# A softmax without its maximum, checked on chip, with a general program behind a branch

## The chip, the cores and the metric

The kernel runs on one core of a Trainium2 chip. A core has a matrix engine (TensorE; PE in the profile, with PEld for its weight loads), a vector engine (VectorE, DVE), an activation engine (ScalarE, ACT), a general one (GpSimd, POOL) and SyncE (SP), which only issues transfers and waits. Each takes its own list of instructions in order; semaphores tie the lists together. SBUF is the working memory (128 partitions), PSUM holds matmul results in eight banks, HBM is the large memory outside.

The metric is the device time of one execution in microseconds (us). The inputs are 8 batches, 8 heads, sequence 1024, head size 64, in float32.

## The reference

An attention whose keys and values are projected along the sequence from 1024 to 64 rows is followed by a token mixer and a channel mixer.

```python
k_proj = einsum('ks,bhsd->bhkd', E, k)          # E, F: 64 x 1024
v_proj = einsum('ks,bhsd->bhkd', F, v)
scores = (1 / sqrt(64)) * matmul(q, k_proj^T)
scores = scores - max(scores, axis=-1)
attn = exp(scores)
attn = attn / (sum(attn, axis=-1) + 1e-09)
x = matmul(attn, v_proj)                        # heads side by side: 1024 x 512 per batch
h = relu(x^T @ w_tok1) @ w_tok2                 # token mixing, 1024 -> 256 -> 1024
u = x + h^T
out = u + relu(u @ w_ch1) @ w_ch2               # channel mixing, 512 -> 1536 -> 512
```

## The kernel before

Matmuls run in bf16. All weights stay in SBUF. The work is a list of 2,203 jobs; a job is one short run of instructions on one engine.

Per batch, the front is: loads of k, q and v from HBM (issued by POOL, `load_heads`, L358); projection of k and v (`kv_proj`, L521); a transpose of the projected k and of q, by TensorE for the first batches and by a transposing DMA on SP for the later ones (L558, L600); scores (`scores`, L637); the exponential on ScalarE straight from PSUM (L652); `attend` (L672), which multiplies the exponentials with the projected v. `vb` holds a column of ones beside v, so the same matmul also yields the row's sum. VectorE takes the reciprocal of the sums into the tile `rdn` (L686) and multiplies it into `x_sb` (L692). The maximum of the reference is never subtracted: mathematically it cancels, as long as the exponentials and their sums stay in float32's range. `rdn_t` is a pair of tiles, one for even and one for odd head pairs, so a slot is used again two head pairs later.

Token mixing follows (`token1`, `token2` for the first batches; `token1_seven`, L857 and L875, and `token2_seven`, L969 to L1027, for the later ones). `token1_seven` and the channel mixing form a 2x2 block product from seven products instead of eight (a Strassen scheme), with VectorE making sums and differences of operand blocks before and after (L857, L807, L1216). `turn_u` transposes u by DMA. Channel mixing runs on half a batch at a time: `up_set` (L1180, three sets a half) and `down_block` (L1289), with additions to the output in L1332 and L1342 and a store by POOL (L1326). The last half has its own ending, `finish` (L1377), with small pieces and stores on SP and ACT.

Channel mixing of one batch runs on TensorE beside the front of the next one.

The order of all jobs is written out. `ORDER` is a string with two characters a job, 64 times the first digit plus the second; `Planner.plan` decodes it, checks that each job's dependencies come before it, and gives each PSUM tile the bank that `SPOTS` names. `FILLS` names places in that list where one extra matmul of zeros (`blank`, L436, reading the tile `zero`) is put in at the start. The launch loop (L1545 on) emits the jobs in that order, and `pin` holds each engine to it. The costs and due times in `pe`, `dve`, `act` are not used when the list is given.

After the last job the framework closes the program (L1557): SP waits for the semaphores of all transfers still on their way, and two barriers of all engines with a clearing of semaphores follow.

Of the kernel before, what the change touches and what calls it, by code (L numbers as in the profile page):

```python
# [15 lines left out]
    "0R030T0Q050P0S0408060U070W0V001L0X011M02091E0A1F1G1I1H1J0B1K1N1j1O0C1P1k1c0D1Z1d1Q1e1g1f1h1i0E1R1S1l"  # L16
    "1T1m1W1X0s1U0H0u0w0t0v1n0z0G0x0+1+0F0y0-201-101a1Y24111b1V26250J1812271B19151A1621130I14281C1D1u291o"
    "172S230K2A2T221p1r1q2N2O1v1s2B1t2E1x2P0M2C2U1w2Q1y2V2F1z2R2X2K2W2D2Y2H2G2Z2a2L2I2c2J2b2d2M2l0L2x2m2h"
    "2y2e3B2f2n2i2g2p2o2z3C2q2t2+2-2u2j2r0O302k332v2s0Y37342w310N3L0Z0a353M3d3I3H3D3v323J3N36383R3O0c3E3P"
    "3e0d4c0e3Q3j3K0g3h0f393F3i0b3S3A3f3T3k0h3g3U3-3l3V3G0i3w3X9w3n3W3Y3z4d3m3x3+4u4Y3y4a3p4v4Z403q4g410k"  # L20
    "4w3o5A424x4y0l5B4e0j4h5p4b4f454j464i4k3r5C4z0m43475D5E4l444-0o4m503s4o4n3t4+4p5q525t514B5F4q5r4C495s"
    "530p544D3Z5y3u5w0q5H3bA15x4J3c3a6B5u5I554K5z4r4G4L5K5v4A4H9v5L9x6D484I5+6E0r6F564M6C5-6G6O4N6A606P6Q"
    "626H6I6L4O636561646Z6J674s666K4EA26a57684F6M6b696N4Q0n6f4P6U6g6R6W4R6S6h6Y4U4S6V6c6i6T6X5S4T6d6j6k6u"
    "6l6e5T6m6n6x6+6v5U6o4V6-6y6z716p5a6q4W5G705b725J746r7A73756s765M6t776wA35N7B5O585Q787C5R4t5X5P795Y7J"
    "7F7K7D7G7H7Q7EA57I5Z7L7R5dA759A85eA65VA95fAAA45W5c5h5g5i7V7S5l7TAD7Z7X4X5m5j7a7n5k5n7b7o7W7d5o9z7M7e"
    "7p9-7c7O7q7g7P7r7h7N7f7sAF7i7uAH7Y7lAG7t7m7v7jAJ837wAIANAK7x84ALAOAhAM7z7yAiAP877kAj857U7+88AQAb8986"
    "ARAS8AAcAdAk8BAWAlAm8L9yAZ8CAYAeAT8DAfAaAg8FAUAXAV8M8G8EENB3At7-Az8N8mAEA+8+8i8n8TA-EO8k8oAuAvABAn8H"
    "8U8pB4B5AC8-8q81B0Aq8r92Ao8J90Ap938QArAs8jB6AwB18tB2B795Ax8uB88R8l91Ay8s96B9948v8w9G978x8yBB9H988SBD"
    "999I8KBE9KBCBF8z8WBGEP8VEQ9L9ABABI9N9BBJBH9O9+8X9JBKBNA0BLBO8Y9QBM829MBPBRBSBV8I8aBWBQBTBk9R80BYBXBl"
    "8bBZBUBn9PBc8OBdBa9SBeBfBpBbBh8PBgBmBiER9CBj8ZBo9YEVES9TBr9ZEUBqET8eBs9aEW8f8c9UBu8d9g9W9E9hEYBtC1Bz"  # L30
    "9dEZC2B-9iBwC59VC3BxC69eC48gC89D8hEbC9Bv9bEdC0Ec9c9FEfEj9fCBEeEgEkElCC9jB+EmEhEi9kEn9XEpEr9lC7EoCFCA"
    "By9nCGEsEtCDEq9oCEEu9mCJCHEvEwExCI9r9pCKCXEyEz9qCLCYCME+CNCZEaE-F09sCaILCOCPF19tIMCbDACREXCcF2F4F3Cd"
    "CQ9uF5CeF6CpCfF7FBDCChCSFCDEF9CqDFFADSCiCgFDCrDICTFEDGDJF8FGCjFHFFDHFLDTFICxCkFMFJFPClDUCmFKDLDBDVFQ"
    "FNDDDMFTCVCyINFUFRFODKCnFWDWFXCuDXDNFYCvCzFaCwFVDZFbDQDaC+DRFiFcDODcFSDPFZFdFfFeIPFjFgDdCUFhFlIRDYIT"
    "DkDbISCsIQCWDlFkIUIOC-CoFmFnDeD0CtFoFpDoFqD2DpD1D3FxIXDmD4D6DnIWFzFsFrDrD5FtDqDsFuF-DtD7G0DfDuD8G1Dv"
    "DwF+G2DgG3E0FvG4E1DiDxFwIZE2DyG6IbD+E8G7DjE9IcDzIdGDEAIaE5FyGEG9DhIeGAE6IfD-IhIgGHIiGFIjGIG5GGIkG8IY"
    "GVInE7GKMKIoGBImEBGCGLIsIlECItIuIpGNIqIrIvGOE3IwEDGWE4IxI-GZJ0EEIyGaEFJ1EGIzI+EJEHGXJ5EIJ2GYGcJ3J4GJ"
    "MJGdHQJ7IVJ9J8GbJAD9H8GfGeJBHCGMJCGhJ6JEH9GPJFGiJDGgJJHAHDJGEKHRGQJHJKGRHGJIGTHEHHMLJLMMJNHSJMHUGSHT"
    "HJHVJOGnJPELHFJRHKGjJTEMHXHBJSGlGoJUGpHIJVHMHLJWHNGsGUHYJYHiJQJZHaJXGtHbHOHjJbHPGvJaHmHWJcHnJgJdGwJe"
    "MNGuJfGxGmHZGyMPGkJhHpHcMOJjMRHkMSMQJkGzHlHdHoHqHeJnGqHrJlJoHsGrMVG+HtHuG-JiJzJmH0J+HvH4JpH1JvJsH2H+"  # L40
    "JtJqH3H-HwJxJ-I0JwH5JrK0K1JyJuHyMXK2HxI6MYHgMaK4HzH6I7MZK5HfKBI3I8KCK7MbHhMcK8KDMdQIMeMfKEKFMgMTMhI4"
    "KGK3I5MiK6KIMmI9KJIAMjMkKLIBMnKMK9MoMpKTMlKHKAKUMqI1MrMsQKIDL7MtKXMuMvKZKYIEKKMwL6KVIFKaL8I2IGMxKbMy"
    "KNKWH7ICKdMzKcKeLgM+LAM-IHLBKON0IIN1N3LEN2KfLFKlKgLON5KmLPIJN7KhIKLCN6N8LHMWN4N9LILSL9QHNAKPLQLDNCMU"
    "KiLRNBNDLKLTNENHKRKnLGKjNFLJLVNGKSKqNILLNJLhLMNKLWKrLNNPNLKtNMNQNNKkLiNOKsNSLkNTLYKuKQLZNWLjQJNUNXKw"
    "LlNVKoKvKpNZNRKxNYLUNaNeNbLnNcQLLXNfNdKyKzLaQMNhQOLbNjLmLoNiK+QNLpQPNgQQK-LcLqL0NlLrL2LeL1LsNmLyLtQT"
    "LzLuNnNoL+L3NtLwNxNkM4NyL4NqO9LxL5M5NvOANwNzNuOBM6N+M1NpOCODNrN-OEM2O0NsQVM3O2QWLvO1LdO3M7QXO4O5QYOG"
    "O7OHM8O8QZOFO6M9QaL-OIQdLfOJOLQeQbOKQfMBOMM0QcMCMAQgMDQlQkMFQmMEQnQhORQjP4QUMGP6QiONQRP8OSQoP7P9OXQS"
    "QpQqOVUGPAMHOWQuUFOTPBQvQwOYOUMIQrPCOZQsQtOjPDOaQxQ+PFQyQzObQ-OdR0OcPMOePGOkPNP5PIR1R5PJR3PEOlOPPOPQ"
    "OfPPOrOhR6PHPROsR4R7R2PTR8PSPURAR9RBOoRCPVOpOgUIRFOQRDRGOqPWREPKOtPXPeRJRHOiPfRKRNRLPYRIROOuPLRQPZUH"
    "PiRRPgRcOOPhRSOvRMRTRPRUOwUJRdRVPjRWPaRXUNRfUKRZRYOyULRaRhUMPlRgRbReUOPmPwRiPkRjPnPxRkOzPcPoOmO+PpRl"  # L50
    "RmPyO-PqRnOnRrRoQ2RtOxRvPrQ3RwRpP0Q4RqP1RxP2S7RyPsRzPuUPPbR+P-UQRuPvURS0RsQ0S8S1UUSBUVQ1S9SCS3UWSAQ5"
    "PdUTUXS4SEUYUZUSR-SDSFS2UaSGQ6UbUdS5Q7SJUePtUfUcQ9UgUhSPT3SHSKSQUoQASIUpS6STT2UrUqSUSRT6UsSSQBSWUlUt"
    "QCSXPzUmT7T4P+UnUiQ8TASZUjUkShSLT8UxUuT9QDUvSaUwSVUzQESYU-SiU+V0TBSbT5QFV1TCSNV2QGTDSjUyV4P3TETcScV5"
    "V3TFSpV6SqSdSOV9SfV7VASeTGTdVDSMTKV8THTeSrTIVHTJVBVISmVETLVFVCSnVKTgVLVMThTMSoVJTfVOVGTjTNVPVWTkTOVQ"
    "TiTPVRTlVTSsVNStVUVXTRVSTmTSSgVZVVTQTnVaTuTTToSuSkTpTWTqSwTXSxTYVdVYSySlTsSzTvVeTUSvVbVlTVVgVpVnS+Vf"
    "VqVcS-TwVmVtT0U0VuVoT1W1VhU1W2TaViVwVjVrVxU2W5VkWJW6VvWKTzVyT+WNT-V-W8W0VzU3WOW9W7VsU4WAV+WQTrWPTZWR"
    "WLWSW3WDU5W4X0TtWBWyWTTbWCXIWMWzWVW+WUTxWEX1TyWFU7U6U8WWX4W-U9UBWXWbUAWZX2XaX3UCX5WcXbUDXJX7WYXcWdWH"
    "X6XdWGXMX8WgXNX9WhXPXCXQXAXDXeWiWjXfWaXOXBXEXKXGWmXRXLWIWkXUWlWnXVXhWoWeXiXWXgWqXjWrXmWfXnXkXoXSWsXs"
    "XTWpWtXtXlXHUEXYWuXZXuXpWvXqXFX-XXX+WwXxWxXyXvY9XzXrY0XwY1Y4Y2Y3Y6Y5Y7YAYDY8YBYCYJYFYEYMYGYKYNYHYLYO"
    "YIYPYQ"  # L60
)
SPOTS = (
    "3024101126436327273643040127120236363170420436171063240217145624732113405063774765765024721257605205"
    "6726211311072323401724223063354705252601467407364317023117417326261333177136413604752570156153207422"
    "0717501237102275300221337643164504125123103737627351104724633607633666334154626574653573657273116524"
    "1713476526117451111000431363504562017414020567306256407306640427552552201753173152014723475602015723"
    "0720475332734202200176315612415716323744645200150524671"
)
FILLS = (21, 21, 21, 21, 21, 21, 21, 27, 27, 30, 36, 36, 36, 36, 49, 62, 62, 66, 66, 79, 79)
WHOLE = 3  # L70
TWO = 2
T1 = 2
T2 = 2
SUMS = 60.0

SINGLE = 2
TOTALS = ((), (0, 1), (2,))
# [12 lines left out]
HWK = 0  # L90
SIDES = "AAADADADADDAAAAAAAAADAAAAAAAA"
FMAX = 3.4028234663852886e38


class Job:

# [1465 lines left out]
```

## Time and profile before

| | us |
|---|---|
| three runs | 416.77, 414.83, 415.90 |
| median | 415.9 |
| the profiled execution | 415.69 |
| its span, first to last instruction | 413.9 |
| PE busy | 406.4 |
| DVE busy | 355.9 |
| ACT busy | 221.9 |
| POOL busy | 66.8 |

The granted TensorE clock was 0.999 of full speed. Busy times of PE are modelled ends of pipelined matmuls, so a busy PE need not be at its peak; where it is, shows in the time per matmul. A DMA's time is from its issue to its landing. Lines are those of the kernel before; `xN` is a count. A wait `A <- B` says that A's engine sat idle until B.

### The profile page before, as it was taken

What the parts mean: (1) busy time and instruction counts of PE and PEld (TensorE: products, weight loads), DVE (VectorE), ACT (ScalarE), POOL (GpSimd) and SP (SyncE); (2) the same over time, 40 slices, a digit from 0 to 9 for tenths busy, and PEclk for the clock granted to TensorE, in tenths of its full rate; (3) what the DMA queues carried; (4) which work ended last, traced back from release to release, by engine and by line L of the source; (5) the groups of instructions that cost most, each with busy time, mean ns of one, the idle gap of its engine ahead of it and who ended that gap; (6) DMA issues with size and microseconds to landing.
All of it is one profiled execution on the core that took longest, in us unless ns stands there. A gap on an engine that the chain in (4) does not pass through costs nothing.

```text
span 413.9 us, 9589 instructions
## 1 busy us (share of the span) xinstructions
PE 406.4 (98%) x3909; PEld 344.4 (83%) x3911; DVE 355.9 (86%) x773; ACT 221.9 (54%) x429; POOL 66.8 (16%) x105
## 2 busy tenths in 40 slices
PE   8899999999999999999999999999999999999996
PEld 4489888688888888979988899888988798998896
DVE  2289899779999999989979798898989899988686
ACT  1647884258635664574754646455644745445520
POOL 8544021021102120112001112012100001010010
PEclk9999999999999999999999999999999999999999
DMA  8999999997998897978966869873996212251115
GB/s 153 205 202 204 207 190 192 160 172 170 189 166 168 201 170 143 166 156 156 245 118 127 133 148 178 143 167 89 180 227 118 52 51 103 52 115 39 52 69 187
DMA packets 93755, 61.69 MB, mean 149 GB/s; under 512 B 59024, under 2 KB 89232, under 8 KB 93712
## 3 DMA queue, kind: packets, MB, share of 16 engines
q0 software_dynamic: 35088, 45.09, 55.7%
q1 hardware_dynamic: 58256, 15.47, 22.8%
q8 instruction: 30, 0.49, 0.5%
q10 hardware_dynamic: 368, 0.52, 0.3%
q14 instruction: 13, 0.11, 0.1%
HBM read 59.24 MB, written 16.78 MB: 184 GB/s over the span
## 4 chain that ended last, share of the span: by engine, by line
PE 92%; DMA 4%; DVE 2%; POOL 1%; issue 1%; POOLq 0%; DVEq 0%
PE psum L1289 36%; PE psum L1180 35%; PE psum L991 5%; PE psum L875 4%; PE psum L672 3%; PE psum L521 3%; DMA q_sb<-in_q_dram 3%; PE psum L637 2%; DMA v_sb<-in_v_dram 1%; PE psum L712 1%; PE psum L1060 1%; PE psum L736 1%; DVE u L1105 1%; PE psum L1092 1%; PE psum L618 1%
## 5 line engine op out<-in xcount | busy, mean ns | idle before, releaser
L1289 PEld LDWEIGHTS <-G 128*128 128x128 bf16 x1356 | 130.0, 98 | 18.3 <-issue 3.5
L1289 PE MATMUL psum<-wc_sb,G 128*128 128x256 bf16 (+1 forms) x780 | 101.5, 271 | 0.0
L1180 PEld LDWEIGHTS <-wc_sb 128*128 128x128 bf16 x768 | 73.9, 98 | 10.5 <-issue 2.1
L1202 ACT ACTIVATE G<-psum 128x512 bf16<-128x512 f32 x96 | 56.2, 601 | 44.8 <-PE psum L1180 44.3
L1289 PE MATMUL psum<-wT,G 128*128 128x256 bf16 x576 | 75.6, 273 | 0.1
L1216 DVE TENSOR_TENSOR G<-G 128x512 bf16<-128x512 bf16 (+1 forms) x140 | 69.4, 515 | 0.8
L1180 PEld LDWEIGHTS <-wT 128*128 128x128 bf16 x576 | 55.3, 98 | 7.3 <-issue 0.6
L1180 PE MATMUL psum<-S,wc_sb 128*128 128x256 bf16 x384 | 56.2, 273 | 0.0
L1180 PE MATMUL psum<-S,wT 128*128 128x256 bf16 x384 | 56.0, 273 | 0.1
L1180 PE MATMUL psum<-uT,wc_sb 128*128 128x256 bf16 x384 | 55.5, 273 | 0.0
L1326 POOL DMA_DIRECT2D out_dram<-o x30 | 16.4, 548 | 212.7 <-DVE o L1332 171.2
L692 DVE TENSOR_TENSOR x_sb<-psum,rdn 128x256 bf16<-128x256 f32 (+1 forms) x88 | 46.7, 540 | 1.8
L1332 DVE TENSOR_TENSOR o<-psum,u 128x512 f32<-128x512 f32 x59 | 39.9, 681 | 3.7 <-PE psum L1289 3.3
L1208 ACT COPY ub<-psum 128x512 f32<-128x512 f32 x48 | 28.1, 588 | 23.4 <-PE psum L1180 18.5
L652 ACT ACTIVATE a<-psum 128x512 bf16<-128x512 f32 x64 | 34.9, 603 | 8.5 <-PE psum L637 8.3
L1161 DVE CUSTOM_DVE_ANT_0 G<-psum,ub 128x512 bf16<-128x512 f32 x48 | 32.7, 683 | 6.9 <-PE psum L1180 6.6
L1223 ACT COPY psum<-psum 128x512 f32<-128x512 f32 x48 | 27.6, 579 | 18.6 <-PE psum L1180 13.0
L1161 DVE CUSTOM_DVE_ANT_0 G<-psum,ua 128x512 bf16<-128x512 f32 x48 | 32.6, 684 | 5.3 <-PE psum L1180 4.4
L1208 ACT COPY ua<-psum 128x512 f32<-128x512 f32 x48 | 28.3, 590 | 14.0 <-PE psum L1180 13.6
L1180 PE MATMUL psum<-uT,wT 128*128 128x256 bf16 x192 | 28.7, 273 | 0.0
L358 POOL DMA_DIRECT2D v_sb<-in_v_dram x18 | 13.3, 742 | 75.4 <-PE psum L1180 22.7
L672 PE MATMUL psum<-vb,a 128*128 128x130 bf16 x256 | 25.3, 220 | 0.0
(102 smaller groups left out, 499.4 us busy)
## 6 DMA issues: line engine op xcount, KB each, us to landing
out_dram<-o POOLq DMA_DIRECT2D x30, 512.0 KB, 3.8
k_sb<-in_k_dram POOLq DMA_DIRECT2D x14, 512.0 KB, 11.2
v_sb<-in_v_dram POOLq DMA_DIRECT2D x14, 512.0 KB, 7.3
q_sb<-in_q_dram POOLq DMA_DIRECT2D x14, 512.0 KB, 9.2
wc_sb<-in_moe_w_ch_dram POOLq DMA_DIRECT2D x6, 256.0 KB, 11.9
wc_sb<-in_moe_w_ch_dram POOLq DMA_DIRECT2D x4, 384.0 KB, 13.3
k_sb<-in_k_dram POOLq DMA_DIRECT2D x4, 256.0 KB, 7.9
q_sb<-in_q_dram POOLq DMA_DIRECT2D x4, 256.0 KB, 8.1
```

Source lines behind the costliest of these rows:

```text
L652: lambda g=g, half=half, bk=bk: nc.scalar.activation(out=a_t[g][:, half], in_=bank(bk), func=ACT.Exp, scale=scale),
L672: nc.tensor.matmul(view()[:, k, c].rearrange("p i d -> p (i d)"), a_t[g][:, c, at : at + P], vb[:, g].rearrange("k i d -> k (i d)"), start ...
L692: lambda: nc.vector.tensor_tensor(out=x_sb[:, rows, g * P : (g + 1) * P].rearrange("p (n c) (i d) -> p n c i d", c=2, i=2), in0=view()[:, ...
L991: nc.tensor.matmul(view(X_OF[n])[:, r, :], tok2_of(n, i, r), T[n] if n in T else h[B[n]], start=(n in (1, 7) and r == 0), stop=True, skip_ ...
L1161: nc.vector._custom_dve(TENSOR_ADD_SAT, out=out, in0=in0, in1=in1, s0=FMAX, s1=0.0)
L1180: nc.tensor.matmul(t[:, c, :], w1_of(n, dd, 2 * m + c), a_of(j, n, dd), start=(n in (1, 7) and c == 0 and dd == 0), stop=(c == 1 and dd == 1),
L1202: lambda: nc.scalar.activation(out=G[:, n, cs], in_=view(src), func=ACT.Relu),
L1208: 512, lambda: nc.scalar.copy(out=dst, in_=view("y")), writes=[(name, s % 2)],
L1216: 512 * len(both), lambda: f(out=G[:, n, c], in0=G[:, a, c], in1=G[:, b, c]), ps=False,
L1223: 512, lambda: nc.scalar.copy(out=view("y"), in_=view("x")), takes=[bk["y"]],
L1289: nc.tensor.matmul(to, G[:, G_OF[n], cc, t * P : (t + 1) * P], w2_of(n, cc)[:, cut], start=(n in opens and (t == 0 or alone) and cc == 0), ...
L1332: 512, lambda: nc.vector.tensor_add(out=dst, in0=view(src), in1=u_of(sh, dh)),
```

## The change

1. The reciprocals of the sums get one tile with a slot for each head pair of two batches (`rdn_t`, 8 slots; the slot is counted by `attended`), so all reciprocals of a pair of batches stand side by side: 128 partitions x 128 values.
2. `extremes(n)`, once per pair of batches, reduces them to their maximum and minimum on VectorE. The results, and all that follows, lie in the tile `zero`, which the fills read at the start.
3. Near the end of the list, four small VectorE jobs compare the four maxima with 2^100 and the four minima with 2^-100, and add up to one vote per partition; a matmul of one column adds the votes of the partitions, and VectorE copies the number into `flag` as an integer. A column of ones for that matmul is written early.
4. After the whole list every engine loads `flag` into a register (`values_load`) and branches: where it is above 0, `general()` computes everything again with the row maximum subtracted, one head at a time, fully unrolled. For the given inputs no sum leaves the range, and the branch is not taken.
5. `ORDER`, `SPOTS` and `FILLS` are new strings for the 2,217 jobs (14 more). The loads' sizes, the tiles and all other jobs are the same.

```diff
-FILLS = (21, 21, 21, 21, 21, 21, 21, 27, 27, 30, 36, 36, 36, 36, 49, 62, 62, 66, 66, 79, 79)
+FILLS = (11, 11, 22, 22, 22, 22, 22, 22, 33, 33, 33, 33, 33, 42, 42, 42, 61, 70, 70, 82, 82, 92)
...
+BIG = 2.0**100
...
-    rdn_t = [tile_of([P, NJ, 2, 2], F32, f"rdn{i}") for i in range(2)]
+    rdn_t = tile_of([P, 2 * HP, NJ, 2, 2], F32, "rdn")
...
+    small, votes = zero.bitcast(F32), zero[:, 124:126]
+    ends, flag = small[:, 0:16], small[0:1, 60:61].bitcast(mybir.dt.int32)
...
+    attended = iter(range(2 * B * HP))
+
+    def extremes(n):
+        for i, op in enumerate((ALU.max, ALU.min)):
+            dve(
+                8 * HP * NJ,
+                lambda i=i, op=op: nc.vector.tensor_reduce(
+                    out=ends[:, 4 * i + n : 4 * i + n + 1], in_=rdn_t.rearrange("p a b c d -> p (a b c d)"),
+                    axis=mybir.AxisListType.X, op=op,
+                ),
+                reads=[("rdn", at, jj) for at in range(2 * HP) for jj in range(NJ)], writes=[("ends", n, i)],
+                ps=False, prio=0.0,
+            )
+
     def attend(g, half, due, span):
+        at = next(attended) // 2 % (2 * HP)
...
-            rdn = rdn_t[g % 2][:, 2 * half + jn[0] : 2 * half + jn[0] + n]
+            rdn = rdn_t[:, at, 2 * half + jn[0] : 2 * half + jn[0] + n]
...
+        if b % 2:
+            extremes(b // 2)
...
+    dve(
+        4,
+        lambda: nc.vector.tensor_single_scalar(out=ends[:, 8:12], in_=ends[:, 0:4], scalar=BIG, op=ALU.is_gt),
...
+        lambda: nc.vector.scalar_tensor_tensor(
+            out=ends[:, 12:16], in0=ends[:, 4:8], scalar=1.0 / BIG, in1=ends[:, 8:12], op0=ALU.is_lt, op1=ALU.add
+        ),
...
+        lambda: nc.vector.tensor_reduce(
+            out=votes[:, 0:1], in_=ends[:, 12:16], axis=mybir.AxisListType.X, op=ALU.max
+        ),
...
+    dve(1, lambda: nc.vector.memset(votes[:, 1:2], 1.0), writes=["one"], ps=False, prio=0.0)
+    bb = Bank("D", full=False)
+    pe(
+        1, 64, lambda: nc.tensor.matmul(bank(bb)[0:1, 0:1], votes[:, 0:1], votes[:, 1:2], start=True, stop=True),
+        reads=["votes", "one"], takes=[bb], prio=0.0,
+    )
+    dve(
+        1, lambda: nc.vector.tensor_copy(out=flag, in_=bank(bb)[0:1, 0:1]), writes=["flag"], uses=[bb], prio=0.0,
+    )
...
+    def general():
...
+        for b in range(B):
+            for src, to in ((k, k_sb), (v, v_sb), (q, q_sb)):
+                nc.gpsimd.dma_start(out=to, in_=src[b].rearrange("h (p si) d -> p h si d", p=P))
+            for h in range(H):
...
+                nc.vector.tensor_reduce(out=top, in_=s_ps, axis=mybir.AxisListType.X, op=ALU.max)
+                nc.vector.tensor_tensor(out=e, in0=s_ps, in1=spread(top), op=ALU.subtract)
+                nc.scalar.activation(out=e, in_=e, func=ACT.Exp, scale=scale)
...
+    bad = nc.values_load(flag[0:1, 0:1], min_val=0, max_val=2 * P)
+    with tc.If(bad > 0, preferred_fallthrough_block=False):
+        general()
```

In the new list the check's jobs stand as follows (place in the list of 2,217, and the time at which their neighbours ran before): the column of ones at 140 (28 us); the reductions of batches 0 and 1 at 464 and 490 (80 to 87 us), of 2 and 3 at 893 and 1024 (155 and 180 us), of 4 and 5 at 1503 and 1547 (272 and 278 us), of 6 and 7 at 1876 and 1879 (340 to 341 us); the comparisons and the vote at 1885 to 1892, the matmul at 1896 and the flag at 1898 (up to 346 us).

## The prediction

> **What bounds the kernel now.** I read the page first: its busy line, instruction queues and DMA issues.
>
> ```profile
> PE 406.4 (98%) x3909; PEld 344.4 (83%) x3911; DVE 355.9 (86%) x773; ACT 221.9 (54%) x429; POOL 66.8 (16%) x105
> ...
> q8 instruction: 30, 0.49, 0.5%
> ...
> q14 instruction: 13, 0.11, 0.1%
> ...
> out_dram<-o SPq DMA_DIRECT2D x2, 128.0 KB, 2.2
> ```
>
> TensorE is nearly always busy. The two instruction queues fetch program code while it runs: q8 in packets of 0.49 MB / 30 = 16 KB, q14 in packets of 0.11 / 13 = 8 KB. The time of one packet is its share of 16 engines' span: 0.005 x 16 x 413.9 / 30 = 1.1 us on q8, and likewise 0.001 x 16 x 413.9 / 13 = 0.5 us on q14.
>
> Next the windows, for where TensorE is short of work (columns: PE, PEld, DVE, ACT and POOL busy, each with its count).
>
> ```profile
> 0.00:25.00 25.00, 20.97 (x182) 11.52 (x183) 8.51 (x33) 11.61 (x24) 16.08 (x29) 1.00 1.04 185
> 340.00:350.00 10.00, 10.00 (x93) 8.91 (x92) 9.85 (x21) 5.21 (x12) 1.06 (x2) 1.00 0.27 107
> 360.00:380.00 20.00, 20.00 (x186) 18.03 (x184) 16.96 (x33) 8.98 (x17) 1.07 (x2) 1.00 0.44 96
> 380.00:400.00 20.00, 20.00 (x186) 17.94 (x184) 15.00 (x28) 7.77 (x15) 0.53 (x1) 1.00 0.07 28
> 410.00:414.00 4.00, 0.62 (x12) 0.44 (x8) 0.90 (x3) 0.00 (x0) 0.00 (x0) 0.86 0.61 199
> ```
>
> From 380 to 400 us, 183 matmuls of 256 columns run at 20 / 183 = 0.109 us each with no idle, and the waits of PE between 30 and 410 us are an empty list. So the middle is TensorE work and nothing else. Only the first 25 us, which wait for data, and the last 3 us are open. What the start waits for (waits of the weight loads, 0 to 30 us):
>
> ```profile
> PEld L618 <- DMA q_sb<-in_q_dram: 2.5, 3, 0.9
> ...
> PEld L574 <- DVE kb L334: 1.1, 2, 0.6
> ...
> PEld L521 <- DMA k_sb<-in_k_dram: 0.7, 1, 0.7
> ```
>
> Last the end, from the timeline and the closing line L1557.
>
> ```profile
> 409.24 2.07 SPq L1326 DMA_DIRECT2D out_dram<-o  x3
> ...
> 410.32 0.62 DVE L1377 TENSOR_TENSOR o<-psum,ub 128x128 f32<-128x128 f32 x2
> ```
> ```profile
> L1557 SPq EVENT_SEMAPHORE  x11: 17/28/28, 411.4 to 413.8; - x11
> ...
> L1557 SPq DRAIN  x3: 7/7/13, 413.1 to 413.4; - x3
> ```
>
> TensorE and VectorE are done by 410.9 us. SP has issued the last store at 411.3, then waits on nine lines of semaphores for landings until 413.1, and two barriers of all engines take the last 0.8 us. Between 411.3 and 413.1 there are 1.8 us of pure landing: cover for anything SP does meanwhile.
>
> **The sum starts from** the profiled execution's own 415.69 us (span 413.9, 1.8 around it), 0.2 below the median of 415.9.
>
> **The sums kept apart.** The reciprocals go to one tile with 8 slots per pair of batches, not 2. No instruction is added; a wait for reuse goes that VectorE's own order had met already: 0.
>
> **VectorE's new work.** Eight reductions of 128x128 f32. Bounds: the MEMSET of that size at L303, 165 ns; the two-input addition of that size at L1377, 288 ns. I take 0.25 us, 2.0 us in all. Three operations on 128x4 cost a RECIPROCAL of that form (L686, 170 ns), 0.5 us together; the copy of one element lies between the 64x4 MEMSET (62 ns) and the 64x64 CAST (228 ns), I take 0.17; the MEMSET of a column is 0.06. In the new list the reductions of batches 0 to 5 stand about 80, 87, 155, 180, 272 and 278 us, where VectorE has 1.4 to 2.7 us idle in the 10 us that follow (one place, 155, has 0.1): hidden, and each worth 0.25 if not. The last two, with the check behind them, stand between the last attention multiply (340.6) and the four subtractions of L857 that token mixing's products wait for. That is 0.5 + 0.5 + 0.17 = 1.2 us, in a window where VectorE is busy 9.85 of 10. It comes back only after 360, where 3 of 20 us and then 5 of 20 are free. Next late are those subtractions and then TensorE's L875. Bounds 0 and 1.2; since today's equally full window makes PE wait for nothing, the low end is nearer: 0.3.
>
> **TensorE's new work.** One weight load (98 ns) and one matmul of one column, 0.13 us in line. It waits for VectorE's votes, with a single product of 0.44 us between the two in the list; bounds 0 to 0.7, taken with the row above as 0.
>
> **The order anew.** The loads, their sizes and nearly their sequence stay: the first q is that of heads 4 and 5, then v and k of heads 2 and 3. The third landing still opens the first projection, and the twelfth the end of the start. The SP transposes and all closing products keep their places but for neighbours; one POOL store of batch 6 goes behind a later one, and no tile waits for it near the end. TensorE's work is the same sum. 22 fills stand for 21, 0.2 us each and placed where it idles. I take 0; bounds from the waits shown: 2.5 us of q gone, or as much again.
>
> **The branch.** Every engine, when its own list is done, reads the flag into a register, compares, skips the general program and meets the closing waits. No row shows such a read: bounds are the 17 ns of a semaphore event and the 2.0 us of the shortest landing (L1326); I take half of the latter, 1.0, as a round trip without a store's descriptors. What is skipped is long. Counted from the diff, TensorE has 48 matmuls per head, 64 heads, and 256 per batch: 5,120, with weight loads 10,240 records; at 0.49 MB for today's 7,820 that is 0.64 MB, 40 packets of q8. VectorE has about 770, SP 64 stores and their waits. So the code behind it is not the next page, and I expect each engine to fetch a page once, with nothing to do. Bounds 0 (already there) and 2.2 + 1.1 (a store's landing and a q8 packet); I take 1.0 for the trip and the packet on top. SP: 411.3 + 1.0 + 0.1 + 1.0 + 0.5 = 413.9, then nine waits that are all met, 28 ns each at least and some 0.06 apart when met, 0.5: 414.4 against 413.1, so +1.3. TensorE: 410.9 + 1.0 + 0.1 + 1.0 + 1.1 = 414.1, +1.0, beside it. I put the end at +1.4. If the cover of the last landing were gone, it would be 3.1 in place of 1.4.
>
> The Trainium skill, page "Runtime: NRT & Kernel Launch", section "Instruction fetch mechanics", says that fetching is sequential and hidden, and that a taken branch whose target is not in the two-page window stalls for the fetch. The trace agrees with the first half: 30 fetches on q8 and no PE wait from 30 to 410 us; no run here shows the second. By that rule the stall is paid, as in the forecast; without it the first rival holds. The page's "TENSOR_LOAD ldr" of about 200 ns per register would, as an estimate, make the sum 0.8 smaller.
>
> **Sum:** 415.7 + 0.3 + 0.13 + 0 + 1.4 = 417.5 us, +0.4% on the median. Its own range, with the order at +-1 and the page at +-0.8, is 416.1 to 419.2.
>
> **The rivals.**
> - *The skip is free*: the code that follows is already fetched. SP is through at 411.3 + 1.1 = 412.4, before the last landing, and only part of the met waits shows, 0.3. Time 416.4. For it: the branch asks for the skipping side to stand next. Against: the general program must lie somewhere between here and the end of the stream.
> - *The start gets shorter*, not slower than before: the new list lets the projections meet their data so that the 2.5 us for q go. 417.5 - 2.5 = 415.0. It decides from 1.6 us gained. Against: the landings set the start and their number is the same.
> - *The end pays in series*: a fetch into the skip, semaphores that the untaken part would have raised made up after the last landing at 413.1, a second fetch at the closing code. 413.1 + 2 x 2.1 + 0.3 + the 0.8 of barriers = 418.4 of span against 413.9; time 415.7 + 4.5 + 0.4 = 420.6. For it: 40 pages are skipped, and closing waits count every landing. Against: nothing in this trace.
> - *VectorE's 1.2 us falls on PE* in full: 417.5 + 0.9 = 418.4, counted in the forecast's spread.
>
> **How the numbers follow.** Half a per cent, 2.1 us, is what a measurement of this kernel can tell from no change: limits 413.8 and 418.0. Forecast 0.46, of which 0.19 above 418.0 and 0.27 within. Skip free 0.17: 0.16 within, 0.01 faster. Shorter start 0.12: 0.07 within, 0.05 faster (with a free skip, 413.9 or less). In series 0.25: 0.24 slower, 0.01 within. Together faster 0.06, same 0.51, slower 0.43. The range that leaves out a tenth on each side goes from 415.0, the shorter start, to 420.8, just above the series.
>
> **What would show it.** After 410.9 us each engine's last own work is followed by a gap of about 2 us before L1557's counterparts; a q8 and several q14 packets lie in it; SP's waits then stand close together. The span's end moves from 413.9 to 415.3. Eight reductions of 0.2 to 0.3 us; no PE wait over 0.3 us at 340 to 360; the first attention projection still near 9.9 us and the first L1180 near 34. The prediction is wrong if TensorE's last matmul moves by more than 1 us from 410.6 in either direction, or if the gap at the end exceeds 3 us.

## The result, and the profile after

The changed kernel takes 419.82 us (419.43 to 419.89) against 415.58 us for the kernel before in the same session: a ratio of 1.0102, 95% interval 1.0082 to 1.0121. It is slower by 1.0%, 4.2 us. The forecast was 417.5, +0.4%; the range of 415.0 to 420.8 holds the time.

The profile page of the changed kernel, its busy line and its two instruction queues:

```profile
PE 406.1 (97%) x3910; PEld 344.1 (82%) x3913; DVE 357.6 (86%) x786; ACT 221.1 (53%) x429; POOL 66.8 (16%) x105
...
q8 instruction: 32, 0.52, 0.5%
...
q14 instruction: 19, 0.16, 0.1%
```

TensorE's busy time is the same within 0.3 us (406.4 before), VectorE's grows by 1.7 us with 13 more instructions. From here on a page is one packet of program code: two more are fetched on TensorE's queue q8 (32 for 30) and six more on q14, which serves the other engines (19 for 13). So the new time is not work.

The same windows as in the prediction (PE, PEld, DVE, ACT and POOL busy, each with its count, then TensorE's clock, DMA share, GB/s):

```profile
0.00:25.00 25.00, 21.64 (x206) 12.63 (x207) 9.85 (x38) 11.48 (x24) 16.83 (x30) 1.00 1.07 188
340.00:350.00 10.00, 10.00 (x92) 8.75 (x91) 9.83 (x26) 4.79 (x11) 1.60 (x3) 1.00 0.41 159
...
380.00:400.00 20.00, 20.00 (x185) 17.92 (x184) 14.05 (x25) 9.27 (x17) 1.53 (x3) 1.00 0.14 54
410.00:414.00 4.00, 0.00 (x0) 0.00 (x0) 0.14 (x1) 0.00 (x0) 0.00 (x0) 0.78 0.36 111
```

The middle is as full as it was. At 340 to 350 us, where the check stands, TensorE still has no idle time. In the last window TensorE does nothing at all, where it did 0.62 us before: the work is through earlier, not later. VectorE's last operations by the timeline (start, us):

```profile
409.52 0.62 DVE L1397 TENSOR_TENSOR o<-psum,ub 128x128 f32<-128x128 f32 x2
```

They end at 410.14 us, 0.80 before their old end of 410.94, and yet the span ends 4.1 later, at 418.0. Everything lost is lost between 410 and 418 us, with no engine computing. What stands there is the branch (line L1679 of the changed kernel) and the closing code (L1706):

```profile
L1679 SPq EVENT_SEMAPHORE  x8: 17/17/17, 411.1 to 413.6; - x8
...
L1679 PEldq COMPARE_BRANCH  x2: 95/1972/3848, 408.9 to 410.0; - x2
L1679 DVEq COMPARE_BRANCH  x2: 51/53/55, 410.5 to 410.7; - x2
```
```profile
L1706 SPq EVENT_SEMAPHORE  x14: 17/28/28, 414.3 to 417.9; - x14
...
L1706 ACTq DRAIN  x2: 8/58/108, 414.3 to 417.7; - x2
L1706 DVEq DRAIN  x2: 11/34/57, 414.3 to 417.7; - x2
L1706 ACTq EVENT_SEMAPHORE  x2: 17/17/17, 415.3 to 417.9; - x2
...
L1706 DVEq EVENT_SEMAPHORE  x2: 21/21/21, 417.6 to 417.9; - x2
```

(Columns: count, shortest, median and longest in ns, first and last start.) TensorE's jump over the general program takes 3.85 us. VectorE and ScalarE jump at 410.7 and do nothing until 414.3. The arm is the general program, which isn't taken. In its place SP raises the eight semaphores that the arm's stores would have raised (the x8 above), and the last of these waits until 413.6 for the last store of the kernel itself. Then the two barriers: ScalarE is past the first at 415.3, VectorE only at 417.6. The DMA issues near the end (409 to 418 us; KB each, median us from issue to landing) add the last piece:

```profile
out_dram<-o SPq DMA_DIRECT2D x2, 128.0 KB, 2.9
out_dram<-o ACTq DMA_DIRECT2D x1, 128.0 KB, 1.9
```

The two SP stores, 2.2 us in the median before, take 2.9. The last of them alone (DMA from 410 to 418 us) takes 3.5, with eight code packets beside and behind it:

```profile
q14 instruction: 6, 0.05, 2.5%
q8 instruction: 2, 0.03, 2.1%
...
out_dram<-o SPq DMA_DIRECT2D x1, 128.0 KB, 3.5
```

Read part by part from the landings, the last store has 15 of its 16 parts in place at 411.92 and the sixteenth at 413.63. Before, all sixteen came together at 412.99.

### The profile page after: what moved, and what is told of

Same layout as the page of the kernel before. It is cut to its first block, busy times and chain, and to the rows that moved or that the text cites. A ratio compares the mean times of both kernels' runs of the same rounds, so it can differ in the third digit from the quotient of the medians.

```text
span 418.0 us, 9640 instructions
## 1 busy us (share of the span) xinstructions
PE 406.1 (97%) x3910; PEld 344.1 (82%) x3913; DVE 357.6 (86%) x786; ACT 221.1 (53%) x429; POOL 66.8 (16%) x105
## 4 chain that ended last, share of the span: by engine, by line
PE 93%; DMA 2%; POOL 2%; DVE 1%; issue 0%; POOLq 0%; DVEq 0%
PE psum L1309 35%; PE psum L1200 35%; PE psum L1011 5%; PE psum L895 4%; PE psum L692 4%; PE psum L525 3%; DMA k_sb<-in_k_dram 2%; PE psum L641 2%; PE psum L1112 1%; PE psum L732 1%; PE psum L756 1%; PE psum L1080 1%; PE psum L622 1%; POOL v_sb L362 1%; POOL k_sb L362 1%
## 5 line engine op out<-in xcount | busy, mean ns | idle before, releaser
L1309 PE MATMUL psum<-wc_sb,G 128*128 128x256 bf16 x780 | 100.9, 271 | 0.0
```

The lines of the kernel that those rows point to most:

```text
L1309: nc.tensor.matmul(to, G[:, G_OF[n], cc, t * P : (t + 1) * P], w2_of(n, cc)[:, cut], start=(n in opens and (t == 0 or alone) and cc == 0), ...
```

## The experiments

Two theories stood against each other at first. **The far skip** (theory A in the expectations): what costs is the fetch of code behind the jump. **The new list and the check:** the order, the eight reductions and the flag's way through TensorE cost the time somewhere and the end only shows it.

### The list and the check alone

The new list without check and branch, and the new list with the whole check but without register read, branch and general program:

```
-        lambda: nc.vector.tensor_single_scalar(out=ends[:, 8:12], in_=ends[:, 0:4], scalar=BIG, op=ALU.is_gt),
...
-        1, 64, lambda: nc.tensor.matmul(bank(bb)[0:1, 0:1], votes[:, 0:1], votes[:, 1:2], start=True, stop=True),
...
-    bad = nc.values_load(flag[0:1, 0:1], min_val=0, max_val=2 * P)
-    with tc.If(bad > 0, preferred_fallthrough_block=False):
-        general()
```
```
-    bad = nc.values_load(flag[0:1, 0:1], min_val=0, max_val=2 * P)
-    with tc.If(bad > 0, preferred_fallthrough_block=False):
-        general()
```

> The new order, banks and fills for the 2,203 old jobs alone: without the 14 jobs of the check and without the branch (the sums' tile with its eight slots stays). Theory A: the start gains what it gained in the changed kernel, 0.5 to 1.3 us of work ahead, and the check's matmul and its wait (0.24 us of TensorE at 342 us) are gone: 414.4 to 414.9 us, within 0.5 us of the kernel without the branch. Theory B: the check's reductions on VectorE cost over 1 us, so this one is that much faster than the kernel without the branch.

> The changed kernel with its new order and its whole check up to the flag, but without the register loads, the branch and the general program (the flag is left unread). Theory A, all of the loss lies behind the last own work, in the skip over the general program: the work ends as in the changed kernel (VectorE's last at 410.1 us) and the old closing of 2.9 us follows, so a span near 413.1 and a time of 414.9 us, 0.7 below the kernel before. Theory B, the check's VectorE work and the new order cost part of it: above 416 us.

Measured: 415.09 us, ratio 0.9995 (0.9981 to 1.0009), and 415.26 us, ratio 0.9994 (0.9984 to 1.0003). Both lie 0.2 to 0.4 us above what theory A expected and under the 416 of theory B. The list and the check cost nothing that can be measured. The loss needs the branch.

### A near skip

The branch as it is, with a general program of six instructions in place of the whole one, which is left out:

```
     def general():
...
+        nc.gpsimd.dma_start(out=wt1_sb, in_=w1t)
+        nc.tensor.matmul(banks[0][:, 0:P], ident, ident, start=True, stop=True)
+        nc.vector.tensor_copy(out=x_sb[:, 0, 0:P], in_=banks[0][:, 0:P])
...
```

> The changed kernel with a general program of only six instructions (it leaves out the rest of that program, which these inputs never run), so the register loads, the branch and the semaphores made up in its place stay but nothing far is skipped. Theory A, the far skip costs through its page fetches: no engine is held 3.5 us at the branch, the last store's sixteenth part lands with the others near 412.2 us, VectorE is not held 2.3 us between the barriers; what stays is SP's work after the last landing, 1.0 to 1.4 us. Time 415.7 to 416.3 us. Theory C, the branch itself costs, however far it goes: 418.5 us or more.

Measured: 414.91 us, ratio 0.9984 (0.9974 to 0.9993). This is 0.8 us less than theory A expected, since SP, with one semaphore to raise in place of eight, has passed ten of its twelve closing waits when the last store lands. Register read, compare and closing waits are all there, and free. The whole 4.9 us, 419.82 - 414.91, belong to what is skipped: its length, and the seven semaphores more.

### The branch without the new list

The kernel before, with a flag that is always zero, the branch and the whole general program (the check is left out):

```
+    flag_t = tile_of([1, 1], mybir.dt.int32, "flag")
+    nc.vector.memset(flag_t, 0)
...
+    bad = nc.values_load(flag_t[0:1, 0:1], min_val=0, max_val=2 * P)
+    with tc.If(bad > 0, preferred_fallthrough_block=False):
+        general()
```

> The kernel before with its old order and no check, but with a flag that is zero from the start, the register loads, the branch and the whole general program behind it. Theory A: the closing grows as in the changed kernel. Without VectorE's second fetch (the place of the page's edge is another one) 415.6 + 2.6 = 418.2 us, with it 420.4. Theory B, the loss comes from order and check: below 416.5 us.

Measured: 418.67 us, ratio 1.0076 (1.0059 to 1.0093). The branch alone gives three quarters of the loss. Its trace has the holds of 3.3 to 4.0 us, but not the 2.3 us of VectorE between the barriers. The suspicion was that the rest depends on where the code happens to lie.

### VectorE's second page, and SP's waits

64 more VectorE instructions inside of the general program, which never run and only move VectorE's closing code; and, apart from that, the general program's stores on POOL's queue, so that SP has nothing to skip:

```
+        for i in range(64):
+            nc.vector.memset(ub_t[1][:, 0, i : i + 1], 0.0)
```
```
-                    nc.sync.dma_start(out=out_v[b, :, NJ * i + jj], in_=to)
+                    nc.gpsimd.dma_start(out=out_v[b, :, NJ * i + jj], in_=to)
```

> The changed kernel with 64 small VectorE instructions added inside the general program, where they are never run: they only move VectorE's closing code by half a page of 128 instructions. Theory A, VectorE's hold of 2.3 us between the barriers is a second page fetched on demand, because the code it jumps to ends a page: the hold goes, 419.8 - 2.1 = 417.7 us (417.2 to 418.3). Theory D, the hold is what a far skip costs this engine wherever the page's edge lies (its fetch queue is shared): 419.4 us or more.

> The changed kernel with the general program's stores issued by POOL in place of SP, so SP has next to nothing to skip and no semaphores to make up after the last landing, and its closing waits run beside it. Theory A: SP is ready some 0.8 us sooner, but VectorE's second page comes at the same time as before, so next to nothing is gained: 419.3 to 419.9 us. Theory E, the delays at the end stand one behind the other and add up: 1.0 to 1.4 us gained, 418.5 us.

Measured: 417.88 us, ratio 1.0058 (1.0040 to 1.0076), for the first. Its closing code (L1708), as above:

```profile
L1708 ACTq EVENT_SEMAPHORE  x2: 17/17/17, 415.5 to 416.2; - x2
L1708 DVEq EVENT_SEMAPHORE  x2: 21/21/21, 415.6 to 416.2; - x2
```

VectorE passes the first barrier with the others, and 1.94 us are gone, by instructions that never run. What fits this is that in the changed kernel VectorE's closing code crosses the edge of an instruction page a few instructions behind the jump's target, and VectorE waits for one more page. That the place of the code decides is shown; the page itself isn't, since three packets pass on q14 near 415 us in both kernels and the trace doesn't say for which engine. The second kernel took 419.96 us, 1.0120 (1.0063 to 1.0176): SP goes on 0.2 us after its jump, but VectorE's second page still ends last, so nothing is gained.

### Loops, to make the arm shorter

The general program as a loop over the eight batches (TensorE skips about 1,300 instructions); the same with its stores on POOL; and the latter with 64 matmuls that never run, to move TensorE's closing code by half a page:

```
-        for b in range(B):
+        with tc.For_i(0, B, 1) as b:
...
-                nc.gpsimd.dma_start(out=to, in_=src[b].rearrange("h (p si) d -> p h si d", p=P))
+                nc.gpsimd.dma_start(out=to, in_=src[bass.ds(b, 1)].rearrange("o h (p si) d -> p (o h) si d", p=P))
```

> The changed kernel with the general program as a loop over the eight batches in place of eight copies: VectorE, ScalarE, SP and POOL then skip less than a page or two, TensorE about 1,280 instructions, still five pages. Theory A: VectorE and ScalarE are not held, TensorE is held 3.8 us from 410 us, which ends with the last landing and costs little. If TensorE's own fetch is what delays the last store (16th part at 413.6), SP's work after it follows: 417.5 us. If the other engines' fetches delayed it, 416.5 us. Theory C, the branch costs by itself: 419 us or more.

> The loop over batches and the stores by POOL together. Theory A: SP has no semaphores to make up after the last landing. With a landing delayed by TensorE's fetch 416.4 us, without it 415.8 to 416.5, set by TensorE's arrival at 413.9 us; in any case above the short program's 414.9, because one far skip stays.

> The general program as a loop over the batches with its stores on POOL, and 64 more matmuls (128 instructions of TensorE) ahead of that loop, which never run: they only move TensorE's closing code by half of a 256-instruction page. Theory A (in the two loop variants the time around the span grew from 1.8 to 2.8 and 3.5 us because TensorE's closing code crossed a page's edge just behind the jump and waited there for a second page): without that edge 1.8 us lie around the span again; TensorE is still held by its skip for 3.5 to 4 us and the last store's sixteenth part is still late, so the span stays near 415.6 and the time is 417.2 to 417.8. Rival (what lies around the span has nothing to do with where TensorE's code stands): as the loop with POOL's stores, 418.7 to 419.9.

Measured: 419.45 us, 1.0102 (1.0077 to 1.0126); 419.09 us, 1.0087 (1.0066 to 1.0108); 417.17 us, 1.0051 (1.0033 to 1.0069). VectorE goes on 0.6 us after its jump in all three, TensorE only after 3.8 to 4.1 us. In the first two the time was missed: the span is short (415.8 and 415.6 us), but 2.8 and 3.5 us lie around it in place of 1.8. TensorE fetches a second page in them, at 414.8 and 415.2 us; if its closing code needs that page, the execution ends only after it. The shift of half a page takes the extra time away again (1.5 to 1.6 us around the span in all six executions), as was expected of it, although a page still comes at 414.8: so that TensorE waited for it in the other two is argued, not seen. By its ratio this is the fastest form found that keeps the whole general program and the check, though only level with the 1.0052 further down: some 2 us better than the change as given, still 2.1 behind the kernel before.

Two forms with more loops were to bring the skip near (over batch, head and half; and over the channel tiles as well), and the second was also run with the bound of the check at 2**-20, so that the general program runs:

```
+            with tc.For_i(0, H, 1) as h:
+                for src, to in ((k, k_sb), (v, v_sb), (q, q_sb)):
+                    one = src[bass.ds(b, 1), bass.ds(h, 1)].rearrange("o h (p si) d -> p (o h) si d", p=P)
+                    nc.gpsimd.dma_start(out=to[:, 0:1], in_=one)
```

> The general program written as loops over batch, head and half (each head's rows are loaded by themselves, each half of u is copied to one place first), so that TensorE skips about 400 instructions where the change as given has it skip 10240. Theory A (the skip costs where its target lies outside of the pages that an engine holds; a page is 256 instructions of TensorE): 400 instructions are more than one page and fewer than two, so this one lies at the edge: either nothing is fetched ahead of the last landing (414.9 to 415.5, as with the short arm), or TensorE is held by 3.5 to 4 us and the sixteenth part lands late (417 to 418). Rival (what is paid depends on the arm's being there with waits and stores of its own, not on its length): 417.5 to 419.5.

> The same with loops inside of the half as well (over the channel tiles and the output rows): TensorE skips about 300 instructions. Theory A: the target lies in the page behind the branch's own, which is held; no engine is held at its skip, no instruction fetch lies between the last store's issue and its landing, all sixteen parts land within 1.2 us, the span ends near 413.4 to 414.0 and the time is 414.8 to 415.6, no different from before by over 0.3%, with the general program kept whole. Rival (every skip past a whole page is fetched anew): TensorE held 3.5 to 4 us, 417 to 418.

> The same kernel with the bound of the check set to 2**-20 in place of 2**100, so that every sum lies outside of the range and the general program runs: it computes everything a second time, in loops with a load per head and no overlap that was planned. Both theories: no bearing on the skip; the time is some 1000 to 2500 us (8 batches of 8 heads at 6 to 15 us each, and 16 halves at 40 to 80 us).

Measured: 418.13 us, 1.0071 (1.0043 to 1.0100); 418.32 us, 1.0072 (1.0055 to 1.0090); 2864 us. The second miss was one of counting. Every loop brings reset code of its own on every engine, and counted with it in the built program TensorE skips 475 instructions in the one and 425 in the other, not 400 and 300. The branch stands near the end of a page of 256, so both targets lie beyond the next page; both were held for 4.1 to 4.2 us. The general program costs 2,450 us where it runs, in one execution, at a granted clock of 0.65.

### An early fetch

The branch turned round, so that it jumps where nothing is out of range, and an instruction that announces this jump, on four engines some 170 TensorE instructions ahead (64 never-run VectorE instructions are in both kernels):

```
+    hint_at = len(plan) - 40
...
+        if place == hint_at:
+            tc.mark_branch_hint_location("skip", hint="LikelyTaken", engines=(mybir.EngineType.PE, mybir.EngineType.DVE, mybir.EngineType.Activation, mybir.EngineType.SP))
...
-    with tc.If(bad > 0, preferred_fallthrough_block=False):
-        general()
+    with tc.If(bad < 1, preferred_fallthrough_block=False, label="skip") as fits:
+        pass
+    with fits.Else():
+        general()
```

> The change with its whole general program (TensorE skips over 10000 instructions, VectorE has the 64 extra ones that never run, so that its closing code stands clear of a page's edge), the branch written so that it jumps when no sum is out of range, and one more instruction on TensorE, VectorE, ScalarE and SP forty jobs before the end, some 170 instructions of TensorE ahead of the branch: a hint that this branch will be taken. Theory A (the loss is the fetch of the page behind a jump whose target no engine holds): the fetches move ahead of the last stores, none lies between the last store's issue and its landing, no engine is held over 0.5 us at its jump, all sixteen parts land within 1.3 us, the span ends near 413.4 and the time is 414.8 to 415.8, no different from before by over 0.2%. Rival (what is paid is the jump, the waits that are made up at it, or the arm's being there): as the same kernel without hints, 417.3 to 418.5.

> The same kernel without the four hints. Both theories: TensorE held by 3.5 to 4 us at its jump, the sixteenth part late, no second hold of VectorE: 417.3 to 418.5, as with the 64 extra instructions alone (417.9).

Measured: 418.50 us, 1.0068 (1.0051 to 1.0084), and without the hints 417.70 us, 1.0052 (1.0031 to 1.0073). A miss, and an instructive one. The jumps with the hints (L1685), then without (L1681):

```profile
L1685 PEldq COMPARE_BRANCH  x1: 413/413/413, 409.3 to 409.3; - x1
...
L1685 ACTq EVENT_SEMAPHORE  x1: 17/17/17, 414.3 to 414.3; - x1
L1685 DVEq EVENT_SEMAPHORE  x1: 21/21/21, 414.5 to 414.5; - x1
```
```profile
L1681 PEldq COMPARE_BRANCH  x1: 3636/3636/3636, 409.0 to 409.0; - x1
```

On TensorE the hint did what it says: a page came at 402.9 us, and the jump took 0.41 us instead of 3.64. This shows that the hold is the fetch. It isn't TensorE's granted clock, which falls in the tail of the changed kernel (0.81 from 411 to 413 us): without the hint it was 1.00 there, and the jump was held all the same. But on the three other engines it did nothing: no page passed on q14 between 363 and 407 us, and VectorE and ScalarE stood until 414.5 and 414.3. And when TensorE entered its early page at once, it asked for the page behind that one, at 411.16 us. The last three stores then had fifteen parts at 411.2, 411.7 and 412.7, and their sixteenth at 413.48, 413.80 and 414.11, one after the other. Without the hint the last came at 413.00. So a fetch costs twice: the engine that waits for it, and the store that is in flight beside it.

### The distance alone

An attempt to move the jump's target across the two-page limit went wrong as well: in the form with loops over batch, head and half, the filling matmuls of the start were cut in three, or in four, to push TensorE's branch further into its page.

```
-                blank(zero)
+                for n, m in ((0, 2), (2, 3), (3, 4)):
+                    nc.tensor.matmul(
+                        banks[5][:, n * P : m * P], zero, zero[:, None, :].to_broadcast([P, m - n, P]),
+                        start=True, stop=True,
+                    )
```

> The general program as loops over batch, head and half (TensorE skips 405 instructions), with each of the 22 filling matmuls of the start cut in three (44 more matmuls, 88 instructions, of the same work): TensorE's branch then stands about 85 instructions into a page of 256 and its target about 490 behind that page's start, inside of the next page, which is fetched when the branch's own page is entered. In the uncut form the branch is some 5 to 10 instructions before a page's end and its target lies a page and a half on. Theory A: no fetch after the last store's issue, TensorE not held, all parts landed within 1.3 us, span 413.4 to 414.2, time 414.8 to 415.8. Rival (a skip of 405 instructions is fetched anew wherever it stands): 417.2 to 419.5, as without the cuts (418.13).

> The same with each filling matmul cut in four (132 more instructions in place of 88): the branch is about 130 instructions into its page, its target about 535 behind that page's start, so one page beyond the next one. Theory A: the fetch and the hold are back, 417.2 to 419.5. Rival (it was the cutting of the filling matmuls, not the place of the target, that helped the other): 414.8 to 415.8, as the other.

Measured: 419.34 us, 1.0096 (1.0073 to 1.0118), and 418.65 us, 1.0067 (1.0043 to 1.0092). TensorE was held for 4.7 us in both. With the loops' own code in the count, the first one's target stands at 63 + 475 = 538, beyond the 512 places of its two pages: neither target was near, and theory A gives both their hold. Nor was the work the same: TensorE finished 0.6 and 0.3 us later than in the uncut form, and with the matmuls cut the output is off by 3.9%, for a reason that stays open. These two decide nothing.

So the short arm was taken again, with nothing added but matmuls that never run, 99 of them (shown) or 199 (the general program is left out, as there):

```
+        for _ in range(99):
+            nc.tensor.matmul(banks[1][:, 0:P], ident, ident, start=True, stop=True)
         nc.tensor.matmul(banks[0][:, 0:P], ident, ident, start=True, stop=True)
```

> The short arm of six instructions (the general program is left out), with 99 more matmuls in it that never run: TensorE's jump passes over 201 instructions in place of 3, every other engine's over the same 2 or 3 as before. The branch stands some 5 to 15 instructions before the end of a page of 256 (the last page was entered at 398.1 us, 250 records before the last), so the target lies inside of the page behind it, about 60 instructions before that one's end. Theory A (the page in use and the next one are held, a jump inside of them is not fetched): TensorE not held over 0.3 us, all sixteen parts landed within 1.3 us, time 414.7 to 415.3, as with the short arm (414.91). Theory C (any jump over a page's edge is fetched anew): TensorE held by 3.5 to 4 us, the sixteenth part late, 416.6 to 417.6.

> The same with 199 matmuls (401 instructions): the target lies one page beyond the one that is next. Theories A and C: TensorE held by 3.5 to 4 us at its jump, one 16 KB fetch about 1.2 us after the jump's start, the last store's sixteenth part 1.4 us or more behind the fifteenth, time 416.6 to 417.6, as with the loops whose closing code stood clear of an edge (417.17). Rival (the length of the arm does nothing, its loads, stores and waits do): as the short arm, 414.7 to 415.3.

Measured: 416.77 us, 1.0028 (1.0015 to 1.0040), and 416.86 us, 1.0042 (1.0026 to 1.0058). The jumps (L1593 with 3 instructions skipped, L1595 with 201, L1595 with 401):

```profile
L1593 PEldq COMPARE_BRANCH  x2: 90/135/180, 409.4 to 410.4; - x2
```
```profile
L1595 PEldq COMPARE_BRANCH  x2: 95/202/310, 409.2 to 410.2; - x2
```
```profile
L1595 PEldq COMPARE_BRANCH  x2: 95/2050/4005, 409.0 to 410.0; - x2
```

The hold begins where theory A says: 0.18 us at 3 instructions, 0.31 at 201, inside of the next page, and 4.0 at 401, one page further. But the time does not follow the hold. 201 cost 1.86 us more than 3, without any hold, where theory A had expected nothing (414.7 to 415.3); 401 cost 0.09 more than 201, with 4 us of it. What the first two differ in is a page and a landing (DMA from 410 to 418 us, with 3 and with 201 instructions skipped):

```profile
q14 instruction: 2, 0.02, 0.6%
...
out_dram<-o SPq DMA_DIRECT2D x1, 128.0 KB, 1.8
```
```profile
q8 instruction: 1, 0.02, 1.1%
q14 instruction: 2, 0.02, 0.7%
...
out_dram<-o SPq DMA_DIRECT2D x1, 128.0 KB, 3.6
```

The reading is that TensorE enters the next page, which it holds, and by that asks for the one behind it. This 16 KB fetch starts at 411.41 us, while the last store is on its way: its fifteenth part lands at 412.20 as it should, the sixteenth at 414.00. The store takes 3.6 us in place of 1.8. No engine waits for the page; SP waits for the store.

### The account

From the records of the sequencers and the landings, in us; "tail" is the end of the span less the end of VectorE's last operation:

```
                       VectorE   15 parts  16th    TensorE       VectorE       span    tail   median
                       done      landed    part    jump          jump          end
before                 410.94    412.98    412.99  -             -             413.91  2.97   415.58
short arm, 3           410.56    412.36    412.37  410.42-410.66 411.10-411.31 413.43  2.87   414.91
arm of 201             410.38    412.20    414.00  410.25-410.62 410.93-411.14 414.97  4.59   416.77
arm of 401             410.18    411.95    413.83  410.04-414.11 410.72-410.93 415.00  4.82   416.86
64 VectorE instr.      410.29    412.05    413.79  410.15-414.06 410.83-414.49 416.22  5.93   417.88
the change             410.14    411.92    413.63  410.00-413.91 410.69-414.33 417.96  7.82   419.82
```

Each row is one execution, and from the third on each adds one thing to the row above it. The fetch beside the last store: 4.59 - 2.87 = 1.7 us. TensorE's hold, nearly hidden behind that landing: 0.2. The other engines' far jumps, with SP's: 1.1, since SP goes on only after the late landing, its next instruction 0.6 us after its jump, and then passes twelve waits that are all met, 0.06 us apart. VectorE's second page: 1.9. Together that is 7.82 - 2.87 = 4.95 us of tail, and 4.85 against the kernel before; the changed kernel's work ended 0.80 earlier in this execution, which leaves the 4.05 by which its span is longer.

Why the sixteenth part is late can be read from the store's own packets, 128 of 1 KB. With 3 instructions skipped all of them start between 411.45 and 411.93 us. With 201 skipped, 120 of them have started by 411.74, and the last eight, one part in sixteen, start only from 412.78 on, as the fetch of 411.41 ends (412.81). In the arm of 401, the kernel with 64 VectorE instructions and the changed kernel the last eight start at 412.64, 412.59 and 412.45, and the fetches end at 412.66, 412.61 and 412.46. So one part of the store stands behind the fetch and waits until it is through. That the two share one of the sixteen DMA engines fits this, but the trace doesn't name the engine of a packet. Why the hint had no effect on q14's engines stays open.

## Why the prediction was wrong

- *Start of the sum* (415.69, 0.2 below the median): right.
- *Sums apart, 0; VectorE's new work, 0.3; TensorE's flag, 0.13; order anew, 0 with 2.5 to either side:* a little too high together. With all of them the kernel stands at 0.9994 of the old time, interval 0.9984 to 1.0003, so the 0.43 were -0.7 to +0.1 us. That is small beside what failed. The reductions of the last group took 0.28 and 0.29 us where 0.25 was taken. The list of PE's waits between 30 and 408 us is one line:

```profile
PE psum L756 <- issue: 0.2, 1, 0.2
```

- *The rival of the shorter start:* its condition was half met and worth nothing. The start's wait for q shrank, and the median of the list alone is that of before.

```profile
PEld L622 <- DMA q_sb<-in_q_dram: 1.5, 3, 0.7
```

- *The branch, +1.4:* this step failed; the runs put it at 419.82 - 415.26 = 4.6 us against the kernel with the check and no branch (4.9 against the short arm). Its terms: the register read was taken at 1.0 us, with 0.2 as the prediction's other estimate, and took 0.48 to 0.55, between the two. The page, "1.0 for the trip and the packet on top", was taken at 1.5 to 2.1 and held the engines for 3.5 to 3.9; TensorE's packet of 1.41 us begins 1.05 us after the jump's start, which is the trip and the packet that were priced, but the engine goes on only 1.4 us after the packet's end. What decided was the cover: the step let SP's and TensorE's ends run beside "1.8 us of pure landing", as though the landing were a fixed end. The fetch itself moved the landing by 1.7 us. Its remark on what a lost cover costs, 3.1 in place of 1.4, was nearer than the sum.
- *One fetch per engine, "with nothing to do":* wrong for VectorE, if the 1.9 us that half a page of shift took away were a second page. The position of the closing code in its page was not looked at.
- *The skip is free:* true of a skip of a few instructions (0.9984), not of this one. The argument against it in the prediction, that the general program must lie in between, was the right one.
- *The end pays in series, 420.6, chance 0.25:* nearest. Its three parts are there: the fetch into the skip, the semaphores made up by SP up to the last landing, and what fits a second fetch at the closing code, on VectorE. But the time is nearest partly by luck. It laid the first fetch behind the landing, where only 0.7 us of the hold showed (413.6 to 414.3), and it took the landing at its old 413.1 too; the real one, 1.7 late, came at 413.6 and not near 414.4 because the work was done 0.8 earlier. The prediction found "nothing in this trace" for it, but its own q14 rows say how often a page ends; the closing code's distance from an edge could have been a case with a chance of its own.
- *What would show it wrong:* the gap between an engine's last work and its closing code, named at 3 us, was 4.1 on TensorE (409.81 to 413.91) and 4.2 on VectorE (410.14 to 414.33). TensorE's last matmul moved by 0.8, inside of the limit of 1.
- *Its own range, 416.1 to 419.2:* 1 and 0.8 to either side of 417.5 make 415.7 to 419.3 at most. The measured 419.8 lies outside of either, because the branch was missed by 3.2.

The Trainium skill, page "Runtime: NRT & Kernel Launch", section "Instruction fetch mechanics", says that a taken branch stalls where its target lies outside of the current two pages. The runs now agree: 0.31 us with 201 instructions skipped, 4.0 with 401. But this stall was not the larger part here: with the last store covering it, it cost 0.1 to 0.2 us, and the fetch beside that store 1.7 to 1.9.

## What to carry to other kernels

A rarely taken arm costs what its instruction fetch runs into, not the length of the jump: at the end of a kernel that is the last store's landing, which every closing wait needs. Let the code behind the last store stay on the page that the engines already execute, and count an arm's instructions with what loops and waits add to them. Before crediting a wait as cover, ask whether the new work uses the same queues as what is waited for.

## What the runs showed of the hardware that was not expected

- One 16 KB instruction fetch beside a 128 KB store delayed one part in sixteen of it by 1.7 to 1.9 us in the kernels of the table, and the other fifteen landed on time. The part's packets started as the fetch ended. In other kernels of this case it was 1.1 to 2.5 us, at times with a second part late.
- TensorE, held by a far jump, goes on 3.6 to 4.7 us after the jump's start, of which the packet is 1.0 to 1.7 us.
- Instructions that never run changed the time by up to 2 us in either direction: 64 on VectorE gained 1.9, 128 on TensorE gained 1.5 by the ratios (1.0087 to 1.0051), 198 on TensorE cost 1.9 (414.91 to 416.77).
- A branch hint brought TensorE's page 7 us ahead and cut its jump to 0.41 us, and made the kernel 0.8 us slower.
